# Strassen's seven half products for the output matmul of an attention and gated-MLP kernel

## The chip, the cores and the metric

The kernel runs on one core of one Trainium2 chip. The metric is the device time of the whole kernel in microseconds (us), taken as the median of several executions. Names used below: PE is the matmul engine (PEld is its loading of weights), DVE the vector engine, ACT the scalar engine, POOL the GpSimd engine, which here issues most loads, and SP the engine that issues stores and transposes by DMA. SBUF is the working memory, PSUM the accumulator memory of eight banks that PE writes.

## The reference

Attention with eight heads, three of which look at all earlier positions and five at a window of 64 and the first four positions, and then a gated feed-forward layer with a gated residual:

```python
# q, k, v: (4, 8, 768, 64) float32
scores = (q @ k.T) / 8, masked: causal for heads 0, 2, 6;
         causal and (window of 64, or key < 4) for heads 1, 3, 4, 5, 7
x = softmax(scores) @ v                    # as (3072, 512)

g   = gelu(x @ w_gate)                     # (512, 1536)
val = x @ w_val                            # (512, 1536)
ffn_out = (g * val) @ w_out                # (1536, 512)
res_gate = sigmoid(x @ w_res)              # (512, 512)
out = x + res_gate * ffn_out               # (3072, 512) float32
```

## The kernel before

The 3072 tokens are worked through in six chunks of four tiles of 128 tokens. Each chunk has an attention part (scores into PSUM, exponent on ACT, masks on DVE, weighting with v on PE, normalisation on DVE), a gate/value part, and an output part. The output part of one chunk is issued between the pieces of the next chunk's attention, so that PE always has something to do. The program is laid out by a list scheduler in the kernel's own Python: operations are added to a graph with a priority, and the scheduler decides the order on each engine and where the semaphore waits go. `HINTS` overrides single priorities, so a change of `HINTS` is a change of order.

The products are done in fp16 with fp32 accumulation. The gate/value part keeps its features transposed (features on the 128 partitions, tokens along the row), in a buffer `hT` of 12 feature blocks by 512 tokens, of which there are two:

```python
P_st = Pool(many("qks", 2, [128, 4096], FP16))     # raw q and k
P_er = Pool(many("er", 2, [128, 4608], FP16))      # exponents, heads with full attention
P_h = Pool(many("hT", 2, [128, NF, 512], FP16))    # features, NF = 12
P_ot = Pool(many("otile", 5, [128, D_MODEL], FP32))
# PSUM: kind: (how many at a time, banks)
    "av1": (3, one(0, 1, 6)), "av2": (1, [(0, 1)]),          # weighting
    "sc": (2, [(2, 3), (4, 5)]),                             # scores
    "gv": (4, one(6, 7, 5, 4, 3, 2)), "out": (2, one(6, 7)), # gate/value, output

# gate/value, for each feature block f (g and v: 4 matmuls of 512 columns each)
matmul(g[:, :], lhsT=w_gate[:, ci, f*128:(f+1)*128], rhs=xT[:, ci, :])   # ci = 0..3
matmul(v[:, :], lhsT=w_val [:, ci, f*128:(f+1)*128], rhs=xT[:, ci, :])
act:  gact = Gelu(g)
dve:  hT[:, f, :] = (gact * 0.5) * v
...
# output, for each of the chunk's four token tiles lt
matmul(rb, lhsT=xT[:, ci, s], rhs=wr[:, ci, :])            # residual gate, 4 x 512 columns
act:  sr = Tanh(0.5 * rb)
matmul(fb, lhsT=hT[:, fi, s], rhs=wo[:, fi, :])            # 12 x 512 columns
dve:  otile = (sr + 1) * fb                                # "gated"
dve:  otile = otile + xtok[:, lt, :]                       # "add"
sp:   out[rows] = otile
```

The last tile of the last chunk does its output product in column slices of 256, 128 and 128, so that its gating and store can begin earlier. While the first data are on their way, PE runs matmuls on a blank tile (line 1178), as many as the scheduler finds time for.

Of the kernel before, what the change touches and what calls it, by code (L numbers as in the profile page):

```python
# [4 lines left out]
NHEAD = 8  # L5
SEQ = 768
# [8 lines left out]
NCB = D_MODEL // 128  # L15
# [24 lines left out]
DT_FIRST = 2  # L40
DT_ALL = 9
# [5 lines left out]
    "0:-96.05 3:-32.5 13:-14.98 398:-205.14 399:-3161.01 400:-242.48 401:-60.67 406:194.11 428:585.68 "  # L47
    "430:523.84 442:461.16 444:1172.07 587:-105.78 592:-108.69 613:396.07 617:407.42 620:-11.7 640:556.2 "
    "642:106.88 643:194.09 646:-2979.21 649:-102.44 659:511.02 686:-2.88 687:77.5 695:496.52 696:499.45 "
    "698:-3129.77 703:60.14 704:-184.95 705:-133.38 707:183.02 708:380.49 711:7.46 712:149.85 713:-50.64 "  # L50
    "715:-14.97 722:1121.95 725:480.98 726:449.69 731:-39.24 732:60.67 733:-318.24 737:-43.72 738:419.39 "
    "739:143.85 743:67.93 744:-230.75 746:-318.2 749:428.99 755:137.07 756:5.66 757:60.69 761:-9.34 "
    "762:495.92 764:2489.99 778:1098.32 789:2479.4 791:2501.2 807:953.41 837:1156.8 842:1419.06 877:2567.99 "
    "879:1563.79 880:2429.98 883:2507.13 898:1013.73 933:1964.55 937:1029.47 939:1471.24 940:2476.14 "
    "955:3421 962:3506.26 963:3575.25 971:3584.03 984:2490.73 989:3565.66 1020:3589.17 1022:2520.47 "
    "1036:2494.69 1066:3486.98 1103:3422.44 1109:3530.5 1114:4315.61 1115:4410.02 1124:-926.78 1134:4596.47 "
    "1141:3465.41 1143:2510.98 1146:2495.35 1152:4653.43 1157:112.2 1170:3039.97 1193:107.93 1248:3488.54 "
    "1265:3479.95 1266:4395.47 1271:4430.01 1272:4484.04 1275:-26.92 1284:5420.01 1289:3472.11 1290:4444.38 "
    "1293:-34.14 1295:3453.61 1302:4490.78 1305:3510.02 1316:3998.02 1318:3550.85 1319:3550.87 1320:4107.35 "
    "1349:3529.55 1351:5429.99 1355:3583.42 1414:5485.04 1451:1066.16 1462:4552.31 1474:4473.03 1475:6343.89 "  # L60
    "1480:4497.31 1530:6505.9 1534:2349.36 1556:5501.98 1602:6498.99 1637:6513.87 1670:7448.62 1687:7406.44 "
    "1689:5504.27 "
# [399 lines left out]
def build_kernel(nc, q, k, v, w_gate, w_val, w_out, w_res, out):  # L462
# [15 lines left out]
    P_st = Pool(many("qks", 2, [128, 4096], FP16))  # L478
# [5 lines left out]
    P_er = Pool(many("er", 2, [128, 4608], FP16))  # L484
# [5 lines left out]
    P_h = Pool(many("hT", 2, [128, NF, 512], FP16))  # L490
# [7 lines left out]
        "av1": (2, one(0, 1)), "av2": (1, [(0, 1)]), "av1": (3, one(0, 1, 6)),  # L498
        "sc": (2, [(2, 3), (4, 5)]), "scr": (3, one(5, 4, 3, 2)), "scr0": (3, one(5, 4, 3, 2)),
# [148 lines left out]
    def loads_rows(c, si, b, a, z):  # L648

        n = z - a  # L650
        BB = batch(b)
        st = Buf(P_st)
        lo, hi = a * 128, z * 128
        base = {0: -60, 1: -15, 2: 50}[c]
        groups = ((0, 4), (4, 8)) if c == 0 else ((0, 8),)
        tok = {}

        def sv(j, h0, h1, w):
            return at(st)[:, :].rearrange("p (j h w) -> p j h w", j=2, h=NHEAD)[:, j, h0:h1, 0:w]
        for gi, (h0, h1) in enumerate(groups):  # L660
            for j, src in enumerate((q, k)):
                t = dma("pool", base + 4 * gi + j, (h1 - h0) * n * 0.089,
                        (lambda j=j, h0=h0, h1=h1: lambda: sv(j, h0, h1, n * 64))(),
                        src[b, h0:h1, lo:hi, :].rearrange("h (p j) d -> p h (j d)", j=n), bufs=[st])
                t.late = 1.2 if c else 0.0
                for h in range(h0, h1):
                    tok[j, h] = t
        values(b, a, z, base + (10 if c == 0 else 2), False, c == 0)

        per = 1 if c == 0 or n == 4 else 2  # L670
        for k_ in range(0, NPAIR, per):
            ps_ = ORDER[k_:k_ + per]
            pr = 1000 * c - 492 + ps_[0] if c else 40 * k_ - 205
            for js in (((1,), (0,)) if c == 0 else ((0, 1),)):
                scr = Buf(P_ps, "scr" if c else "scr0")
                items = [(p, jj) for jj in js for p in ps_]

                def tr(e, items=items, scr=scr):
                    return [e.transpose(out=at16(scr)[64 * x:64 * x + 64, (m * n + i) * 128:(m * n + i + 1) * 128],  # L679
                                        in_=at(st)[:, (jj * NHEAD + h) * 256 + i * 64:(jj * NHEAD + h) * 256 + (i + 1) * 64],  # L680
                                        identity=ident[:, :])
                            for m, (p, jj) in enumerate(items) for i in range(n) for x, h in enumerate(PAIRS[p])]
                tt = G.add("pe", c_mm(128, n) * len(items), tr, [t_ident] + [tok[jj, h] for p, jj in items for h in PAIRS[p]],
                           pr, bufs=[st, scr], name="qkT")
                tt.mode = "col"


                def ev(on, p0=ps_[0], scr=scr, j0=js[0], m=len(items)):
                    def fn(e):
                        o = at(BB.qkt)[:, :, :, lo:hi].rearrange("c j (y x) w -> c x (j y) w", x=2)[:, p0 % 2]  # L690
                        m0 = j0 * 2 + p0 // 2
                        o = o[:, m0:m0 + m, :].rearrange("c m (p j) -> c m p j", j=n)
                        i_ = at16(scr)[:, 0:m * n * 128].rearrange("c (m j p) -> c m p j", m=m, j=n)
                        return e.tensor_copy(out=o, in_=i_) if on == "dve" else e.activation(out=o, in_=i_, func=AF.Copy)
                    return fn
                w = n * 128 * len(items)
                t = G.flex({"dve": (c_dve(w), ev("dve")), "act": (c_act(w), ev("act"))}, [tt], pr,
                           bufs=[scr, BB.qkt], name="qkE")
                for p, jj in items:
                    for i in range(a, z):  # L700
                        (BB.ktok if jj else BB.qtok)[p, i] = t

    def loads_natural(c, si, b, a, z):
# [3 lines left out]
        st = Buf(P_st)  # L707
# [4 lines left out]
        for i in range(a, z):  # L712
            for j, src in ((1, k), (0, q)):
                def sv(i=i, j=j):
                    return at(st)[:, (j * 4 + i - a) * 512:(j * 4 + i - a + 1) * 512]
# [25 lines left out]
    def attention(c, segs, xbuf, xtbuf, xtoks, xttoks, l0=0, last=(), ek=None):  # L741
# [6 lines left out]
        for k_, p in enumerate(order):  # L748
# [34 lines left out]
            P.et = Buf(P_er if any(retr) else P_es)  # L783
            P.where, P.ready = {}, {}
            P.off = 0
            for g in range(0, len(banks), 2):
                scores(P, tiles, [t[1:] + (id(t[2]) in lower,) for t in banks[g:g + 2]], g, retr)
            todo.append(P)
# [295 lines left out]
    def gate_value(c, xtbuf, xttoks, halves=()):  # L1084
        h = Buf(P_h)
        toks = []
        ph(c, "table").append(G.add("act", 0.2, lambda e: e.activation(out=scratch[:, :], in_=ident[:, 0:1], func=AF.Gelu),
                                    [t_ident], 1000 * c - 100, fset="gelu", name="table"))
        for f in range(NF):
            pr = 1000 * c + 500 + f  # L1090
            if f < len(halves) * 2:

                ths = []
                for hf, deps in enumerate(halves):
# [11 lines left out]
                        out=at(h)[:, f, s], in0=at(ga)[:, 0:256], scalar=0.5, in1=at(vb)[:, 0:256], op0=ALU.mult, op1=ALU.mult))(),  # L1106
# [12 lines left out]
            for c0 in (0, 2):  # L1119
# [11 lines left out]
                out=at(h)[:, f, :], in0=at(ga)[:, :], scalar=0.5, in1=at(vb)[:, :], op0=ALU.mult, op1=ALU.mult))(),  # L1131
# [4 lines left out]

    TAIL = (slice(0, 256), slice(256, 384), slice(384, 512))

    def output(c, h, htoks, xbuf, xtoks, xtbuf, xttoks):
        segs = [(b, t) for (b, a, z) in CHUNKS[c] for t in range(a, z)]  # L1140
        for lt in range(4):
# [14 lines left out]
            for w in (TAIL if last else (slice(0, 512),)):  # L1156
                fb = Buf(P_ps, "gv" if last else "out")
                n = w.stop - w.start
                for j in range(6):
                    prev_t = G.add("pe", c_mm(n, 2), (lambda fb=fb, s=s, j=j, w=w: lambda e: [  # L1160
                        e.matmul(at(fb)[:, w], lhsT=at(h)[:, fi, s], rhs=wo[:, fi, w], start=(fi == 0), stop=(fi == NF - 1))  # L1161
                        for fi in range(2 * j, 2 * j + 2)])(),
                        [prev_t, wtok["o", j * 2 // 3], wtok["o", (2 * j + 1) // 3]] + htoks[2 * j] + htoks[2 * j + 1], pr,
                        bufs=[fb, h], name="ff")
# [24 lines left out]
    for c, segs in enumerate(CHUNKS):  # L1189
        xbuf, xtbuf, xtoks, xttoks = Buf(P_x), Buf(P_xt), {}, []  # L1190
        halves = []
        if c == 0:
            last, ek = (), Buf(P_ek)
            for l0 in (0, 2):
                halves.append([])
                last = attention(c, [(0, l0, l0 + 2)], xbuf, xtbuf, xtoks, halves[-1], l0, last, ek)
                xttoks.extend(halves[-1])
        else:
            attention(c, segs, xbuf, xtbuf, xtoks, xttoks)
        h, htoks = gate_value(c, xtbuf, xttoks, halves)  # L1200
        output(c, h, htoks, xbuf, xtoks, xtbuf, xttoks)
# [76 lines left out]
```

The softmax here doesn't subtract the row's maximum and nothing guards it: scores larger than these inputs give would overflow.

## Time and profile before

| what | value |
|---|---|
| time, median of 3 | 270.63 us (270.5 to 271.09) |
| span of the profiled execution | 268.8 us |
| granted clock of PE | 1.000 |
| first gate/value matmul | 19.6 us |
| last matmul issued by | 264.6 us |

Lines of the kernel that matter in the profile: 1116 is the gate/value product of 512 columns (1098 the same with 256, in the first chunk), 1146 the residual gate, 1161 the output product, 857 and 948 scores, 981, 991 and 1005 weighting, 1070 and 679 transposes, 1130 the features, 1165 "gated" and 1168 "add".

The slices of the span show a PE that is full from start to end, and DVE and ACT that go up in the attention parts and down in the gate/value parts. Each digit is the busy share of one fortieth of the span in tenths:

```profile
PE   8999999999999999999999999999999999999995
DVE  2698245485264376445476433486145367534344
ACT  3785358783334877136792243984233788233310
```

A matmul's record of 379 ns is the time from its start to its end; several are in flight at once, so the distance between starts has to be taken from the chain or from the timeline. Idle time of DVE and ACT costs nothing by itself.

### The profile page before, as it was taken

How to read it: one execution, taken by the hardware profiler on the slowest of the kernel's cores; microseconds unless marked ns; L12 is line 12 of the kernel's file. 1: busy time of each engine (PE TensorE's matmuls, PEld its weight loads, DVE VectorE, ACT ScalarE, POOL GpSimd, SP SyncE). 2: the span in 40 equal slices, each digit the busy share in tenths (PEclk: the TensorE clock that was granted, in tenths of full speed). 3: DMA queues.
4: the chain of work that ended last, by engine and by line, in shares of the span. 5: the costliest groups of instructions: out<-in, count | busy, mean ns of one | idle time of the engine just before them, and what ended most of it. 6: DMA issues, size and time to landing. Idle time of an engine off the chain costs nothing.

```text
span 268.8 us, 5676 instructions
## 1 busy us (share of the span) xinstructions
PE 264.2 (98%) x2391; PEld 138.7 (52%) x2391; DVE 140.1 (52%) x273; ACT 139.9 (52%) x215; POOL 87.3 (32%) x124
## 2 busy tenths in 40 slices
PE   8999999999999999999999999999999999999995
PEld 7677465465444455444455444555444455444444
DVE  2698245485264376445476433486145367534344
ACT  3785358783334877136792243984233788233310
POOL 8999508995808029894000000000000000000000
DMA  6999999999999999999994100022000113200013
GB/s 86 171 205 207 185 180 228 169 168 187 171 129 187 154 160 185 216 189 125 184 148 134 41 0 0 2 41 96 25 0 0 39 41 80 78 2 0 1 39 120
DMA packets 97562, 29.38 MB, mean 109 GB/s; under 512 B 85504, under 2 KB 93952, under 8 KB 97536
## 3 DMA queue, kind: packets, MB, share of 16 engines
q0 software_dynamic: 70320, 14.69, 65.5%
q1 hardware_dynamic: 27216, 14.33, 27.9%
q8 instruction: 19, 0.31, 0.5%
q14 instruction: 7, 0.06, 0.1%
HBM read 29.36 MB, written 6.29 MB: 133 GB/s over the span
## 4 chain that ended last, share of the span: by engine, by line
PE 93%; DMA 3%; POOL 1%; DVE 1%; issue 0%; POOLq 0%; DVEq 0%
PE ps L1116 44%; PE ps L1161 23%; PE ps L1146 8%; PE ps L857 5%; PE ps L991 3%; DMA va<-in_v_dram 3%; PE ps L1098 3%; PE ps L981 2%; PE ps L1005 2%; PE ps L1070 1%; POOL qks L555 1%; PE ps L948 1%; PE ps L679 1%; PE ps L1178 1%; DVE otile L1168 0%; DVE otile L1165 0%
## 5 line engine op out<-in xcount | busy, mean ns | idle before, releaser
L1130 DVE SCALAR_TENSOR_TENSOR hT<-gact,ps 128x512 f16<-128x512 f16 x68 | 45.8, 686 | 67.4 <-ACT gact L1128 36.6
L1128 ACT ACTIVATE gact<-ps 128x512 f16<-128x512 f32 x68 | 40.1, 597 | 74.0 <-PE ps L1116 72.5
L1116 PE MATMUL ps<-xT,wv 128*128 128x512 f16 x272 | 74.3, 379 | 0.0
L1116 PE MATMUL ps<-xT,wg 128*128 128x512 f16 x272 | 74.1, 379 | 0.0
L1161 PE MATMUL ps<-wo,hT 128*128 128x512 f16 (+2 forms) x312 | 70.4, 363 | 0.0
L1116 PEld LDWEIGHTS ps<-xT,wg 128*128 128x128 f16 x272 | 26.3, 98 | 31.5 <-ACT xT L1077 0.6
L1116 PEld LDWEIGHTS ps<-xT,wv 128*128 128x128 f16 x272 | 26.2, 98 | 30.5 <-DVE hT L1130 0.5
L1161 PEld LDWEIGHTS ps<-wo,hT 128*128 128x128 f16 x312 | 27.5, 98 | 27.0 <-issue 0.7
L873 ACT ACTIVATE er<-ps 128x1024 f16<-128x1024 f32 (+4 forms) x40 | 34.2, 891 | 9.5 <-PE ps L857 9.4
L555 POOL DMA_DIRECT2D qks<-in_k_dram x36 | 28.3, 827 | 32.4 <-DMA qkt<-qks 21.9
L555 POOL DMA_DIRECT2D qks<-in_q_dram x36 | 28.8, 840 | 0.8 <-POOLq L1260 0.8
L1165 DVE SCALAR_TENSOR_TENSOR otile<-srs,ps 128x512 f32<-128x512 f32 (+2 forms) x26 | 16.8, 644 | 16.5 <-PE ps L1161 16.4
L1146 PE MATMUL ps<-wr,xT 128*128 128x512 f16 x96 | 24.7, 379 | 0.0
L555 POOL DMA_DIRECT2D va<-in_v_dram x24 | 21.6, 926 | 2.7 <-PE ps L1005 2.7
L1149 ACT ACTIVATE srs<-ps 128x512 f32<-128x512 f32 x24 | 14.3, 597 | 15.6 <-PE ps L1146 15.3
L1048 DVE TENSOR_TENSOR xtok<-ps,rcp 128x512 f32<-128x512 f32 (+1 forms) x28 | 16.9, 609 | 0.6
L1168 DVE TENSOR_TENSOR otile<-otile,xtok 128x512 f32<-128x512 f32 (+2 forms) x26 | 16.8, 647 | 0.7
L857 PE MATMUL ps<-qkt 64*128 64x64 f16 (+4 forms) x391 | 16.9, 213 | 0.0
L857 PEld LDWEIGHTS ps<-qkt 64*128 64x128 f16 x391 | 9.8, 94 | 9.4 <-issue 3.4
L873 ACT ACTIVATE es<-ps 128x1024 f16<-128x1024 f32 (+1 forms) x14 | 12.6, 898 | 2.9 <-PE ps L857 2.6
L1146 PEld LDWEIGHTS ps<-wr,xT 128*128 128x128 f16 x96 | 8.7, 98 | 10.0 <-issue 0.7
L1178 PE MATMUL ps<-blank 128*128 128x128 f16 x116 | 11.4, 249 | 1.1 <-DVE blank L527 1.1
(70 smaller groups left out, 212.5 us busy)
## 6 DMA issues: line engine op xcount, KB each, us to landing
out_dram<-otile SPq DMA_DIRECT2D x23, 256.0 KB, 2.2
va<-in_v_dram POOLq DMA_DIRECT2D x24, 128.0 KB, 17.0
qks<-in_k_dram POOLq DMA_DIRECT2D x32, 64.0 KB, 11.9
qks<-in_q_dram POOLq DMA_DIRECT2D x32, 64.0 KB, 12.4
wg<-in_moe_w_gate_dram POOLq DMA_DIRECT2D x3, 512.0 KB, 10.3
wv<-in_moe_w_val_dram POOLq DMA_DIRECT2D x3, 512.0 KB, 10.6
wo<-in_moe_w_out_dram POOLq DMA_DIRECT2D x4, 384.0 KB, 22.2
vs<-va SPq DMA_DIRECT2D x4, 260.0 KB, 7.4
```

Source lines behind the costliest of these rows:

```text
L555: return G.add(eng, issue, lambda e: e.dma_start(out_ap(), in_ap), deps, prio, bufs=bufs, dma=cost, name=name, grp=grp)
L857: return [e.matmul(at(scr)[:, oo:oo + w], lhsT=side(BB, low, 1)[half, k0:k0 + 128], rhs=side(BB, low, 0)[half, qq:qq + w], start=True, sto ...
L873: return e.activation(out=o, in_=i_, func=AF.Exp, scale=SM_SCALE)
L1048: t2 = G.add("dve", c_dve(2 * n * 64), lambda e: e.tensor_tensor(out=xview(), in0=avv(0, DHEAD), in1=scale(), op=ALU.mult), [t1] + xdeps, ...
L1116: return lambda e: [e.matmul(at(dst)[:, :], lhsT=w[:, ci, f * 128:(f + 1) * 128], rhs=at(xtbuf)[:, ci, :], start=(ci == 0), stop=(ci == NC ...
L1128: ta = G.add("act", c_act(512), (lambda gb=gb, ga=ga: lambda e: e.activation(out=at(ga)[:, :], in_=at(gb)[:, :], func=AF.Gelu))(), [tg], p ...
L1130: th = G.add("dve", c_dve(512), (lambda vb=vb, ga=ga, f=f: lambda e: e.scalar_tensor_tensor(out=at(h)[:, f, :], in0=at(ga)[:, :], scalar=0 ...
L1146: e.matmul(at(rb)[:, :], lhsT=at(xtbuf)[:, ci, s], rhs=wr[:, ci, :], start=(ci == 0), stop=(ci == NCB - 1))
L1149: ta = G.add("act", c_act(512), (lambda rb=rb, sr=sr: lambda e: e.activation(out=at(sr)[:, :], in_=at(rb)[:, :], func=AF.Tanh, scale=0.5)) ...
L1161: e.matmul(at(fb)[:, w], lhsT=at(h)[:, fi, s], rhs=wo[:, fi, w], start=(fi == 0), stop=(fi == NF - 1))
L1165: t1 = G.add("dve", c_dve(n), (lambda fb=fb, sr=sr, ot=ot, w=w: lambda e: e.scalar_tensor_tensor(out=at(ot)[:, w], in0=at(sr)[:, w], scala ...
L1168: t2 = G.add("dve", c_dve(n), (lambda ot=ot, lt=lt, w=w: lambda e: e.tensor_tensor(out=at(ot)[:, w], in0=at(ot)[:, w], in1=at(xbuf)[:, lt, ...
```

## The change

What it does and what it is for. Take two token tiles as the two rows of a 2 x 2 block matrix, even and odd feature blocks as its columns, and the output weights as a 2 x 2 block matrix of even and odd feature blocks by left and right 256 output columns. The block product then needs eight half products. The change uses Strassen's scheme in Winograd's form, which needs seven, with sums of blocks made beforehand. A half product is 6 matmuls of 256 columns. So a pair of tiles takes 42 matmuls of 256 columns in place of 24 of 512. It is for less work on PE, in exchange for work on DVE and ACT. Nine of the twelve pairs are done so: both pairs of chunks 1 to 4 and the first pair of chunk 5 (`FAST`).

Sums of the weights are made once (four differences, 1536 elements a row each), sums of the features in each chunk (four, in two groups of feature blocks). One of the feature sums, S3, replaces the block it is made from. Two PSUM banks, X and Y, take the seven products; X keeps accumulating products while its partial sums are copied out ("keep"), and the others are added from Y ("plus").

```diff
+FAST = (1, 2, 3, 4, 5)
 HINTS = ( ... every number of it is new ... )

-    P_st = Pool(many("qks", 2, [128, 4096], FP16))
+    P_st = Pool(many("qks", 3, [128, 2048], FP16))
-    P_er = Pool(many("er", 2, [128, 4608], FP16))
+    P_ea = Pool(many("ea", 1, [128, 4608], FP16))
+    P_eb = Pool(many("eb", 1, [128, 2816], FP16))
-    P_h = Pool(many("hT", 2, [128, NF, 512], FP16))
+    P_h = Pool(many("hT", 1, [128, NF, 4, 128], FP16))
+    P_hs = Pool(many("hS", 1, [128, 3, NF // 2, 2, 128], FP16))
+    wt = sb("wt", [128, 4, NF // 2, 256], FP16)
-        "av1": (2, one(0, 1)), "av2": (1, [(0, 1)]), "av1": (3, one(0, 1, 6)),
-        "sc": (2, [(2, 3), (4, 5)]), ...
+        "av1": (3, one(0, 1, 6)), "av2": (2, [(0, 1), (4, 5), (2, 3)]),
+        "sc": (3, [(2, 3), (4, 5), (0, 1)]), ...

+    def sums(c, h, htoks):                       # dve; two groups of feature blocks, 4 + 2
+            t1 = add(0, (0, 1), (1, 1), ALU.add, deps, "s1")
+            t2 = add(1, 0, (0, 0), ALU.subtract, [t1], "s2")
+            t4 = add(2, (1, 0), 1, ALU.subtract, [t2], "s4")
+            t3 = add((0, 1), (0, 0), (0, 1), ALU.subtract, [t1], "s3")   # in place
+    def weight_sums():                           # dve; four differences
+        t1 = add(0, w(0, 1), w(0, 0), tall)
+        t2 = add(1, w(1, 1), wt[:, 0], [t1])
+        add(2, w(1, 1), w(0, 1), tall)
+        add(3, w(1, 0), wt[:, 1], [t2])

+    def output_fast(c, pi, h, htoks, hs, stoks, xbuf, xtoks, xtbuf, xttoks):
+        ... residual gate and Tanh of both tiles, as before ...
+        X, Y = Buf(P_ps, "out"), Buf(P_ps, "out")
+        # a product: 6 x  matmul(D[:, 0:256], lhsT=left(j), rhs=right(j))
+        p1 = product(X, "A11", "B11", True, [])
+        k1 = keep(p1, 0, 0)                      # copy of X to otile, DVE or ACT
+        p2 = product(Y, "A12", "B21", True, [])
+        c11 = plus(p2, k1, 0, 0)                 # otile += Y, DVE
+        p6 = product(X, "S2", "T2", False, [k1]) # on top of p1
+        k2 = keep(p6, 0, 256)
+        p5 = product(Y, "S1", "T1", True, [c11])
+        p7 = product(X, "S3", "T3", False, [k2])
+        k3 = keep(p7, 1, 256)
+        c22 = plus(p5, k3, 1, 256)
+        p4 = product(X, "A22", "T4", False, [k3])
+        p3 = product(Y, "S4", "B22", False, [c22])
+        c12 = plus(p3, k2, 0, 256)
+        ... gated: one piece of 512 (first tile), two of 256 (second tile, one from X);
+        ... add and store as before ...
```

Beside the products, the change has one feature buffer where there were two, one buffer for each kind of exponents, the raw q and k in three smaller buffers (q and k of the first chunk apart), bank pairs of PSUM that scores and weighting share, and a new order throughout.

## The prediction

> **What bounds the kernel now.** I read the page's busy shares first, then the waits of PE, then the chain of waits in order of time, then stretches of the span, and last the groups by form for the durations.
>
> ```profile
> span 268.8 us, 5676 instructions
> PE 264.2 (98%) x2391; PEld 138.7 (52%) x2391; DVE 140.1 (52%) x273; ACT 139.9 (52%) x215; POOL 87.3 (32%) x124
> PE 93%; DMA 3%; POOL 1%; DVE 1%; issue 0%; POOLq 0%; DVEq 0%
> ```
>
> PE is busy 98% of the span and makes up 93% of the chain that ended last. Busy time alone would not settle it, since matmuls overlap; the waits of PE (us in total, times, longest) do:
>
> ```profile
> PE ps L1178 <- DVE blank L527: 1.1, 1, 1.1
> PE ps L991 <- DMA va<-in_v_dram: 0.4, 1, 0.4
> PE ps L679 <- DMA qks<-in_q_dram: 0.2, 1, 0.2
> ```
>
> All three lie in the start. After the first gate product at 19.6 us, PE waits for nobody. So the time is the start (19.6), plus PE's own throughput for 245 us, plus a tail of 4.2 us after the last matmul at 264.6. The chain in order of time (start, us, what) gives that throughput:
>
> ```profile
> 19.59 1.75 PE ps L1098 x16
> ...
> 45.23 0.86 PE ps L1146 x4
> 46.43 0.97 PE ps L1146 x4
> ...
> 231.29 20.72 PE ps L1116 x96
> ```
>
> 96 matmuls of 512 columns in 20.72 us are 215.8 ns each; 16 matmuls of 256 columns in 1.75 us are 109.4 ns each. A run of four 512-column matmuls takes 0.86 us, and 0.97 us where it borders on matmuls that use part of the array: about 0.1 us for a change of array shape.
>
> The room of the vector engine (columns: stretch, us, then busy time and count of PE, PEld, DVE, ACT, POOL), for an attention stretch and for the gate/value stretch after it:
>
> ```profile
> 129.50:148.20 18.70, 18.70 (x203) 9.53 (x202) 12.09 (x23) 11.13 (x16) 0.00 (x0) 1.00 0.98 152
> 148.20:168.90 20.70, 20.70 (x111) 9.37 (x110) 7.92 (x13) 8.15 (x13) 0.00 (x0) 1.00 0.04 13
> ```
>
> DVE has 6.6 us free in the first and 12.8 us in the second; neither it nor ACT is a bound. The mean durations used below (busy us, mean ns):
>
> ```profile
> L1161 PE MATMUL ps<-wo,hT 128*128 128x512 f16 x276 | 67.6, 379 | 0.0
> L1161 PEld LDWEIGHTS ps<-wo,hT 128*128 128x128 f16 x312 | 27.5, 98 | 27.0 <-issue 0.7 <-DVE hT L1130 0.4
> L1165 DVE SCALAR_TENSOR_TENSOR otile<-srs,ps 128x512 f32<-128x512 f32 x23 | 15.8, 686 | 15.7 <-PE ps L1161 15.6
> L1165 DVE SCALAR_TENSOR_TENSOR otile<-srs,ps 128x256 f32<-128x256 f32 x1 | 0.4, 422 | 0.8 <-PE ps L1161 0.8
> L909 DVE TENSOR_TENSOR es<-es,m_win 128x1024 f16<-128x1024 f16 x10 | 6.7, 680 | 4.3 <-ACT es L873 4.3
> L909 DVE TENSOR_TENSOR er<-er,m_causal 128x512 f16<-128x512 f16 x7 | 2.9, 418 | 0.9 <-ACT er L873 0.9
> L1102 ACT ACTIVATE gact<-ps 128x256 f16<-128x256 f32 x8 | 2.9, 382 | 3.5 <-PE ps L1098 3.5
> ```
>
> **What the skill says.** The Trainium skill, "TensorE: Matmul & The Clock Gate", section "Wait — 56ns, not 53.3ns?", gives a warm start-to-start of N/2.4 + 2.5 ns: 215.8 for 512 and 109.2 for 256 columns. The trace agrees (215.8, 109.4), and shows that halving the columns costs almost nothing per column. The same page, "Step-by-step: what each phase is for", has the next weight load run while the matmul before it streams. A load takes 98 ns here, under the 109.4 ns of a half product, and the 16 matmuls at 109.4 ns each had a load of their own: it hides, with 11 ns to spare. "VectorE: DVE Perf Modes", "The perf-mode tier table", puts a two-tensor operation at double rate for 16-bit SBUF operands and single rate for fp32 or PSUM. The trace agrees: 1024 fp16 elements in 680 ns, 512 fp32 in 686. "PSUM — Partial Sum Buffer", "The four PSUM rules", allows a synchronised read of a partial sum within an accumulation group; the change rests on it, and the kernel before has no case of it.
>
> **The change, part by part.**
>
> *Products.* A pair of token tiles takes 2 x 12 matmuls of 512 columns now: 24 x 215.8 = 5.18 us. Seven products of 6 matmuls of 256 columns take 42 x 109.4 = 4.59 us. That is 0.58 us less per pair. Nine of the twelve pairs change (two in each of chunks 1 to 4, one in chunk 5): 378 half matmuls replace 216 whole ones, saving 46.61 - 41.35 = 5.3 us, all on the path. Changes of array shape do not become dearer: in the two instruction orders I count 88 of them after the first gate product before, 90 after.
>
> *Start.* The order of the changed kernel issues 126 matmuls on the blank tile before the first gate product, against 116, and moves 12 small weighting matmuls ahead of it. The identity comes later on POOL, behind a memset and two mask steps. Q, K, V and weight loads keep their sequence in one saturated queue, so they should land as before. Five blank matmuls at 17.79 us end 0.44 us later and one alone takes 0.22, so each further one costs about 0.06 us; ten make 0.6. I put the start at +0.5 us.
>
> *Vector work added.* Sums of features: four of 1024 fp16 elements and four of 512 per full chunk, 4 x 0.68 + 4 x 0.42 = 4.4 us, and 2.8 us in chunk 5 with half the size: 20.4. Four weight differences of 1536 elements, by extrapolation 0.95 us each: 3.8. In the nine pairs 27 adds of 256 columns from PSUM at 0.42: 11.3. Of 27 copies the order puts 17 on DVE (7.1) and 10 on ACT (3.8). Gating in three pieces for two: 9 x 0.15 = 1.4. DVE rises by 44 us to 184 (69% of the span), ACT to about 144. None of this is on the path by itself.
>
> *Tail of the last chunk.* Here no attention work separates the products. By the order: whole product, residual, p1, residual, p6, p2, p7, p5, p4, p3, residual, last tile. Each product of 0.65 us must be followed by a copy or add of its bank before that bank is written again. From the end of PE's issue to the start of the reader is about 0.27 us now (last matmul of a tile issued by 262.2, gating at 262.48); then 0.38 to 0.42, then a wake-up of some 0.04. That is 0.7 us against 0.65 beside it: 0.05 to 0.1 us short, three or four times. The first p1 waits for the bank of the whole product, whose gating stands on DVE behind the seven last feature sums: 0.35 us. The p2 bank waits for the second tanh (0.27 + 0.60 + 0.05 against 0.65): 0.25. The last residual waits for the gating of p4: 0.2. Together about 0.9 us, which is more than the 0.58 that this pair saves.
>
> *One feature buffer.* The next chunk's first feature tile may be written only after the last product that reads the old ones. In the order, at most one product is left when the next gate products start, and those fill PSUM first. Cost: near 0, at most 0.2 us a chunk.
>
> *Shared bank pairs.* PE does not wait for scores or weighting banks before, so more pairs remove no wait; they only give the order room.
>
> *Attention stretches.* From the last feature tile of chunk 1 to the first of chunk 2, DVE's order is 4 sums, 5 copies, 5 adds, 5 masks, 4 reciprocals, 6 normalisations, 5 gatings, 3 residual adds, 1 transpose copy: 18.6 us by the durations above (reciprocal 0.2). PE has about 17.5 us of work there (18.7 less 2 x 0.58), and about 3 us of gate products before DVE's next feature tile: DVE is some 90% full, where it was 12.1 of 18.7. It issues in order, and PE waits for five or six of its results per stretch. I put this at 0.25 us per stretch, four times: 1.0 us, my least certain term.
>
> Sum: -5.3 + 0.5 + 0.9 + 1.0 = -2.9, and 270.6 - 2.9 = 267.7. The order looks laid out so that attention work stands between almost all products, so I lean a little lower: **267.4 us**.
>
> **The rivals.** (a) PE alone: every new wait is filled, and the whole 5.3 us arrives: 265.3. For it: PE's waits are nil now, and the new order interleaves; against it: the last chunk has nothing to interleave with. (b) The vector engine becomes the bound of the attention stretches: one to two us lost in each of four, giving back everything: 270 to 273. For it: 90% full; against it: adds of the residual and the first group of sums can slide into the gate stretch, where DVE has 12.8 us free. (c) Weight loads: 42 instead of 24 per pair. Break-even is 5.18/42 = 123 ns per half matmul; the trace's 109.4 with a load each speaks against it. With 123 the time would be about 273. (d) The start loses more, because the later identity delays the first transposes: up to +1.5.
>
> **Range and chances.** A gain of over 2% needs 5.4 us, more than the whole saving of PE; only a better start could give it. A loss of over 2% needs rival (b) at its worst. Range 265.4 to 270.4: its low end is (a), its high end half of (b).
>
> **What would show it.** PE's half products at 109 ns start to start (right) or above 115 (rival c). The chunk 1 to 4 attention stretches about 1 us shorter on PE; if they are as long as before, with PE waiting for copies and adds, (b) holds. The stretch from the last gate/value matmul to the last matmul no shorter than 12.6 us (from 252.0 to 264.6): the last pair's term. The first gate product after 20 us: the start's term. Wrong altogether if PE waits for feature or exponent buffers at chunk borders.

## The result, and the profile after

| | before | after |
|---|---|---|
| time, median | 270.65 us | 277.11 us (276.67 to 277.44) |
| ratio, 95% interval | | 1.0239 [1.0224, 1.0254] |
| span of the profiled execution | 268.8 us | 274.9 us |

The change makes the kernel 2.4% slower, and the time lies outside the predicted range. The page of the changed kernel, the same lines as before (busy shares, three rows of the forty slices, the chain of waits by engine):

```profile
span 274.9 us, 6145 instructions
PE 262.7 (96%) x2563; PEld 154.7 (56%) x2563; DVE 175.1 (64%) x362; ACT 146.0 (53%) x233; POOL 87.2 (32%) x124
...
PE   7999999999997299999999999999999999999995
...
PEclk9999999999999579999999999999999999999999
DMA  6999999999999999999952120002210004110013
...
PE 81%; DMA 10%; POOL 3%; DVE 2%; SPq 2%; issue 1%; POOLq 0%
```

DVE rose to 64% of the span and ACT stayed at 53%. The new thing is a hole in PE's row in slices 13 and 14 (82 to 96 us), with a dent in the clock at its end (a 5 and a 7 among nines), and a tenth of the chain that is now DMA. The waits of PE (us in total, times, longest):

```profile
PE ps L879 <- DMA q<-qkt: 7.3, 1, 7.3
PE ps L1313 <- DVE blank L538: 1.1, 1, 1.1
PE ps L696 <- POOL ident L524: 0.5, 1, 0.5
PE ps L1013 <- DMA va<-in_v_dram: 0.3, 1, 0.3
```

The last three belong to the start, as before. The first is one single wait of 7.3 us: scores of chunk 2 wait for `q<-qkt`. This is a copy by DMA (line 749) that moves q and k of one head from the upper 64 partitions to the lower ones, for the four tiles of chunk 2; I call it the q6 copy, after its buffer (the expectations below say "Q copy of tile 6" for it). The chain of waits through that stretch (start, us, what; SPq is the queue of instructions on SP, and "issue" is time for which the profile shows no wait):

```profile
64.59 1.74 POOL va L566 x2
66.33 15.79 DMA va<-in_v_dram
...
82.21 0.47 SPq L649
...
82.72 1.61 SPq L741
...
84.37 1.40 SPq L741
...
85.81 1.37 SPq L741
...
87.49 6.85 DMA q<-qkt
94.34 0.35 issue
94.69 1.01 PE ps L879 x10
95.70 1.85 PE ps L1208 x4
97.55 1.28 PE ps L1229 x6
```

From the top down: POOL may load V of batch 2 from 64.6 us, the load lands at 82.1, and only then can SP issue its next instruction, the shift copy of that V (line 649; it moves V by 64 tokens for the window heads). Batches are counted from 0 and hold six tiles each, so this V is the third of four, and chunk 3 is the first to read it, after 138 us. Behind it on SP stand three transposes of q and k (line 741) and then the q6 copy, which is issued at 87.49 and lands at 94.34. SP took its instructions in order and issued nothing from 76.2 to 82.1 us, so everything behind the shift copy stood still, needed or not. The waits of SP's own queue between 58 and 92 us show the block:

```profile
SPq L420 <- DMA va<-in_v_dram: 5.9, 1, 5.9
```

In the kernel before the shift copy of batch 2 stands far behind the q6 copy, and was issued at 92.76: the q6 copy was issued at 80.81, landed at 87.58, and PE read it first at 89.1. The rows of the copy's buffer in the kernel before (after the colon the shortest, median and longest duration in ns, then first and last start), and the time from the copy's issue to its landing:

```profile
L857 PE MATMUL ps<-q x3: 216/279/323, 89.1 to 91.6; 64*128 64x384 f16 x1, 64*128 64x128 f16 x1, 64*128 64x256 f16 x1
L730 SPq DMA_DIRECT2D q<-qkt x1: 667/667/667, 80.8 to 80.8; - x1
...
DMA to landing us min/median/max: 6.8/6.8/6.8
```

So before there was a margin of 1.5 us (89.1 - 87.58). The new order wants the copy at about 87.4, 1.7 us sooner, and has it 6.8 us later.

The last two lines of the chain show a second loss. Four products of 512 columns took 1.85 us (0.97 and 0.86 in the chain before), and a half product 1.28. The clock by stretch (columns: stretch, length, busy time and count of PE, PEld, DVE, ACT, POOL, then the granted clock of PE; the last two are not used):

```profile
89.00:89.90 0.90, 0.00 (x0) 0.00 (x0) 0.90 (x3) 0.00 (x0) 0.00 (x0) 1.00 2.14 148
90.00:100.00 10.00, 5.30 (x44) 2.85 (x45) 1.09 (x3) 3.12 (x4) 5.93 (x8) 0.50 1.72 196
100.20:103.00 2.80, 2.80 (x47) 1.93 (x47) 0.75 (x3) 1.43 (x3) 0.00 (x0) 1.00 1.85 159
```

While PE waits, at 89.9, its clock falls to one half, and it stays there until 100.2: 5.5 us of work at half speed, 2.7 us lost. The Trainium skill, "TensorE: Matmul & The Clock Gate", section "What's actually happening", has the half clock after an idle window of about 3.4 us and the full one after about 3.4 us of sustained work; here the fall comes 2.5 us after the end of the last matmul (87.4), earlier than the page has it, and the recovery after 5.5 us of work.

Where the 6.2 us of span come from, stage by stage. Each row runs from the start of the last gate/value matmul of one chunk to that of the next, read from the traces; the last column, slack2, is the final version of the experiments below (e11):

| stretch, us | before | after | slack2 |
|---|---|---|---|
| start to chunk 0 | 44.85 | 45.19 | 45.90 |
| chunk 0 to 1 | 41.92 | 41.82 | 41.82 |
| chunk 1 to 2 | 42.32 | 51.38 | 42.90 |
| chunk 2 to 3 | 40.76 | 39.76 | 39.76 |
| chunk 3 to 4 | 39.80 | 39.22 | 39.14 |
| chunk 4 to 5 | 41.98 | 40.41 | 40.41 |
| chunk 5 to the end | 17.13 | 17.16 | 17.18 |

One stretch loses 9.06 us; the three after it gain 1.00, 0.58 and 1.57, which is 3.15 together. The rest is under 0.4.

### The profile page after: what moved, and what is told of

It is laid out like the page before. It is cut to its first block, busy times and chain, and to the rows that moved or that the text cites. A ratio compares the mean times of both kernels' runs of the same rounds, so it can differ in the third digit from the quotient of the medians.

```text
span 274.9 us, 6145 instructions
## 1 busy us (share of the span) xinstructions
PE 262.7 (96%) x2563; PEld 154.7 (56%) x2563; DVE 175.1 (64%) x362; ACT 146.0 (53%) x233; POOL 87.2 (32%) x124
## 4 chain that ended last, share of the span: by engine, by line
PE 81%; DMA 10%; POOL 3%; DVE 2%; SPq 2%; issue 1%; POOLq 0%
PE ps L1139 35%; PE ps L1229 15%; DMA va<-in_v_dram 8%; PE ps L1208 6%; PE ps L879 5%; PE ps L1296 4%; PE ps L1013 3%; PE ps L1121 3%; DMA q<-qkt 2%; PE ps L1003 2%; PE ps L1027 2%; SPq L741 2%; PE ps L1281 2%; PE ps L1092 1%; POOL va L566 1%
## 5 line engine op out<-in xcount | busy, mean ns | idle before, releaser
L1139 PE MATMUL ps<-xT,wg 128*128 128x512 f16 x272 | 70.6, 379 | 0.0
L895 ACT ACTIVATE ea<-ps 128x1024 f16<-128x1024 f32 (+2 forms) x24 | 21.0, 915 | 5.9 <-PE ps L879 5.6
L1208 PE MATMUL ps<-wr,xT 128*128 128x512 f16 x72 | 19.3, 396 | 0.0
L879 PEld LDWEIGHTS ps<-qkt 64*128 64x128 f16 x391 | 10.3, 97 | 14.4 <-issue 12.0
L895 ACT ACTIVATE eb<-ps 128x1024 f16<-128x1024 f32 (+3 forms) x16 | 13.3, 858 | 8.9 <-PE ps L879 8.9
L1242 DVE TENSOR_TENSOR otile<-otile,ps 128x256 f32<-128x256 f32 x27 | 11.2, 417 | 10.3 <-PE ps L1229 8.5
L1296 PE MATMUL ps<-wo,hT 128*128 128x512 f16 (+2 forms) x96 | 16.9, 326 | 0.0
L1236 DVE COPY otile<-ps 128x256 f32<-128x256 f32 x17 | 7.1, 420 | 13.9 <-PE ps L1229 13.8
L1229 PE MATMUL ps<-wo,hT 128*128 128x256 f16 x108 | 15.5, 281 | 0.1
L1229 PE MATMUL ps<-wt,hT 128*128 128x256 f16 x108 | 15.1, 273 | 0.0
L1229 PE MATMUL ps<-wt,hS 128*128 128x256 f16 x108 | 14.9, 273 | 0.0
```

Of the source, the lines that this page charges most:

```text
L879: return [e.matmul(at(scr)[:, oo:oo + w], lhsT=side(BB, low, 1)[half, k0:k0 + 128], rhs=side(BB, low, 0)[half, qq:qq + w], start=True, sto ...
L895: return e.activation(out=o, in_=i_, func=AF.Exp, scale=SM_SCALE)
L1139: return lambda e: [e.matmul(at(dst)[:, :], lhsT=w[:, ci, f * 128:(f + 1) * 128], rhs=at(xtbuf)[:, ci, :], start=(ci == 0), stop=(ci == NC ...
L1208: e.matmul(at(rb)[:, :], lhsT=at(xtbuf)[:, ci, s], rhs=wr[:, ci, :], start=(ci == 0), stop=(ci == NCB - 1))
L1229: e.matmul(at(D)[:, 0:256], lhsT=left[l](j), rhs=right[r](j), start=first and j == 0, stop=(j == NF // 2 - 1), skip_group_check=True) for ...
L1242: return G.add("dve", c_dve(256), lambda e: e.tensor_tensor(out=dst(), in0=dst(), in1=at(Y)[:, 0:256], op=ALU.add), [t, k], pr, bufs=[Y, o ...
```

## The experiments

Two theories. **Q:** the changed order put the shift copy ahead of the q6 copy in SP's queue; the wait and the slow clock after it are the whole loss, and with the order mended the predicted gain shows. Against it stands the rival that the products, the single feature buffer or DVE's extra work are what costs (the expectations call it theory V). **D** was formed after the first four runs, because mending the order did not bring what Q says: up to about 140 us, when the last inputs have landed, the DMA engines are busy 90% or more of the time (nines in the DMA row up to slice 20), the needs that DMA feeds have small margins (1.5 us at the q6 copy before), and a PE that has become faster runs into the next of them.

Every edit moves instructions in one engine's order after the scheduler has run; waits are then assigned anew. `behind((a, b), c)` takes a and b out and puts them behind c. Numbers are the program's instruction groups: 476 the q6 copy, 491 the first half of the shift copy, 469, 475, 479 and 495 transposes on SP, 792 an output store, 1065 the DMA transpose of chunk 2's features (`xT`), 961 a residual, 965 and 966 the first half product, 1023 and 1027 the first two score groups of chunk 2. Times of one kernel are given as median and range, as several of these versions vary by some us from execution to execution. The ratios to before leave out executions that lie more than 1.5% above the fastest of the same version, while the medians and ranges take in all. A profile shows one execution, whose time is given where it stands far from the median.

**1. Mend the order on SP** (e2), and the shift copy alone (e1).

```diff
+    behind((491,), 476)     # e1 and e2
+    behind((469,), 475)     # e2
```

> The changed kernel, with two entries of SP's queue moved and nothing else: the early shift copy of the third batch's values goes behind the copy of q and k to the lower partitions, and one late transpose goes back to its place. Theory Q (order in SP's queue): that shift copy waits for values that land at 82.1 us and holds everything behind it; with it moved, the copy of q and k is issued near 80.5 us and lands near 87, when PE needs it. The wait of 7.3 us goes, and with it the slow clock after it (about 2.6 us): 277.1 - 9.9 = 267.2 us, granted clock 1.00. Theory V (the vector engine or the single buffers hold the attention stretches, and the long wait only hides it): most of the time comes back as waits for DVE or for buffers later on, 272 us or more.

> As the run before, but only the shift copy is moved; the late transpose stays late. Its landing at 81.9 us then sets when the copy of q and k can start. Theory Q: issued near 82.0, landed near 88.5, so a wait of about 1 us stays on PE, too short to slow the clock: 268.2 us. Theory V: as above, 272 or more.

e2: 271.97 us (271.5 to 273.71), ratio to before 1.0045 [1.0028, 1.0063]. e1: 271.35 us (268.08 to 274.61, 20 executions), ratio 0.9988 [0.9969, 1.0007]. The 7.3 us wait is gone in both, and with it 5 to 6 us, but both miss their expectation by 3 to 5 us. PE's waits in e2:

```profile
PE ps L1139 <- DMA xT<-x: 3.6, 1, 3.6
PE ps L879 <- DVE hS L1173: 1.4, 1, 1.4
```

The second is still the q6 copy: it landed at 88.39 and PE went on at 88.74, after the same 0.35 us as in the changed kernel, while the DVE sum that is named ended at 88.75, too late to have released it. The first is new: the gate/value products of chunk 2 wait for the transpose of their inputs by DMA. In the chain:

```profile
102.40 10.33 DMA xT<-x
```

It was issued at the same time as before, but landed at 112.73; before it landed at 109.39 and nobody waited. From 113.2 to 116.7 us the clock was then one half, another 1.7 us. (This execution took 273.71 us, the longest of the five.) In the profile of e1 the same transpose took 8.1 us instead of 10.3 and nobody waited for it; that execution had a span of 269.0, and the q6 copy cost 2.0. So Q names the cause of most of the loss in the changed kernel, and is not enough for the prediction's 267.

**2. The same fault in the kernel before** (b1): its shift copy moved ahead of its q6 copy, nothing else.

```diff
+    behind((491,), 479)
```

> The kernel before, with the shift copy put early in SP's queue as in the changed kernel, and nothing of the change. Its values land at 84.0 us there, so the copy of q and k is issued near 89 instead of 80.8 and lands near 95.5 instead of 87.6. Theory Q: PE waits 4 to 7 us for it and loses 1 to 2.5 us more to a slow clock: 276 to 280 us from 270.65. Theory V: the kernel before, with two feature buffers and little work on DVE, has other work for PE and stays within 1 us of 270.65.

280.06 us (279.01 to 280.89), ratio 1.0341 [1.0313, 1.0369]. The first of PE's waits:

```profile
PE ps L857 <- DMA q<-qkt: 7.2, 1, 7.2
```

A kernel without half products, with two feature buffers and DVE at 52%, gets the same wait from that one move and loses 9.4 us. So the order on SP is enough for this loss, without the new products. That the products, the buffer and DVE do not cost is what the later stretches of the table above show, which gain 3.15 us with all of them in place.

**3. Keep PE's clock up during the wait** (e3): 100 matmuls on the blank tile ahead of the waiting scores of the changed kernel.

> The changed kernel with SP's queue as it is, and 100 matmuls on the blank tile put on PE just ahead of the score matmuls that wait (5.6 us of work in a wait of 7.3 us; their result is overwritten). The wait stays. If the slow clock after the wait comes from PE being idle, the clock stays at 1.00 and the 2.6 us of slow matmuls go: 274.5 us. If the clock falls for another reason, 277.1 stays; if the fill delays the scores, it is longer.

278.53 us (277.93 to 281.4), ratio 1.0307 [1.0252, 1.0363]: not faster. In its profile the fill ran from 88 to about 94, a wait of 3.1 us followed, and the clock was one half from 96.5 to 99.9, for 3.4 us in place of 10.2: 1.4 us of work were lost to it instead of 2.7. Less idling, less half clock; the clock did not stay at 1.00, as the fill did not cover the whole wait. But the start was 1.1 us later in that execution, and the q6 copy was issued 1.3 us later and took 8.2 us instead of 6.9 to land. Whether the fill itself delayed it is open; as a remedy it is of no use.

**4. Take the next DMA need away** (e5a, e5b): on top of e2, what transpose 1065 did is done by PE, into banks 2 and 3, with copies by DVE. It is half of chunk 2's inputs: two of four blocks of 128 columns of `x`, each in four token tiles, so eight small transposes (the expectations speak of four blocks of eight). e5b moves one score group as well.

```diff
+    G.prog["sp"].remove(xd)                       # 1065, DMA transpose
+    tp = Task("pe", ..., 4 x transpose(128 columns) into bank 2 or 3, ...)   # twice
+    te = Task("dve", ..., tensor_copy(xT[:, cb, 0:512], bank), ...)          # twice
+    behind((1023,), 966)                          # e5b only
```

> The version with the shift copy and the DMA transpose back in their old places on SP (271.97 us) still lost 3.6 us of PE waiting for the DMA transpose of chunk 2's features (xT) and about 1.7 us of half-speed matmuls after it. Here four of chunk 2's eight feature blocks (those of that one transpose) are transposed by TensorE (eight 128-column transposes, two copies by VectorE) in place of the DMA. Theory D (the first half is paced by the saturated DMA queues; each DMA-fed need that PE now reaches early costs its wait and some half-speed matmuls): the xT wait and its slow matmuls go, 8 transposes cost 0.45: 271.97 - 3.6 - 1.7 + 0.45 = about 267. Rival: the queues are simply full, and another transfer's wait of 2 us or more takes the place of this one: 270 or above.

> As the run before it, and the first scores of chunk 2, which wait for the padded copy of Q of tile 6, are issued behind a residual and the first half product, so that the copy has about 1 us more. Theory D: of the 1.4 us wait at these scores 1 us goes: about 266.0, the sum of PE's own saving without any stall. Rival (the wait only moves to the next need): no better than the run before it, within 0.3 us.

e5a: 273.07 us (272.64, 274.09, 267.86 and 273.5). e5b: 269.36 us (267.63 to 272.75, 22 executions), ratio 0.994 [0.9918, 0.9963]. Both medians miss what D expects, e5a by 6 us and e5b by 3.4; only the lowest executions come near it. Neither profile has a wait for `xT`. In the profile of e5a the q6 copy costs 2.9 us of waiting and then a clock of 0.7 for a slice, in that of e5b 0.6 us and nothing more; that one, at 267.67 us among the shortest of the 22, shows a span of 265.9, 2.8 us under before. The move in e5b was badly chosen: of the two score groups only 1023 went back, while 1027, which reads the same copy, stayed in front, so the copy had hardly more time. How much of the difference between e5a and e5b is the move, and how much is that between executions, in which the copy lands now sooner and now later (90.99 and 87.77 in the two profiles), is not shown.

**5. Less for the queues to carry** (e6): e2 with 8 of the 16 loads of q and k of chunk 3 left out. Chunk 3 is then computed from stale data, so only the time is of use.

> The version with the old SP order (271.97 us), with 8 of the 16 Q and K loads of chunk 3's tiles left out (2 MB or less that the queues carry while chunks 1 and 2 run; the kernel then computes chunk 3 from stale data, so only its time is of use). Theory D: the queues empty sooner, the Q copy of tile 6 and the transpose xT land 1 to 3 us earlier, PE's waits for them shrink: about 269. Rival (landing times are set by the issue order on SP and a fixed latency, not by the load on the queues): unchanged, 272 within 0.7.

268.90 us (267.62 to 272.56), ratio 0.9918 [0.9898, 0.9938], as theory D expects and 3.1 us under e2. The transpose landed at 109.05 in place of 112.73, and nobody waited for it; but of these 3.7 us 2.4 come from an earlier issue on SP (100.01 against 102.40) and only 1.3 from a shorter way to its landing. The q6 copy did not land sooner (89.23 against 88.39), and PE's wait for it was 1.0. So the loads of a chunk whose attention PE reaches only after 130 us cost some 3 us in chunks 1 and 2. Whether they do so by the bytes that they carry, as D says, or by the issues of POOL and SP (POOL had 8 fewer, and SP's transposes waited less for data), this run does not separate.

**6. Without the last chunk's pair** (e7): as e5b, with whole products in chunk 5.

```diff
-FAST = (1, 2, 3, 4, 5)
+FAST = (1, 2, 3, 4)
```

> As the version with transposes on TensorE and later scores, but the last chunk's pair is computed with whole products again, so that four chunks keep the seven half products. Prices the tail: the pair saves 0.58 us of products and paid 0.50 us of PE waits in the trace of the changed kernel, so without it 0.1 us slower, within 0.4. If the prediction's own tail term (0.9 of waits) was right: 0.3 us faster.

271.48 us (268.15 to 274.95), ratio 0.9978 [0.9954, 1.0001]. The medians do not answer the question, as the profile of e7 (273.38 us) has 2.8 us of waiting for the q6 copy and that of e5b 0.6. The end of the span, behind all DMA waits, says more: from the last gate/value matmul to the end e7 needs 17.53 us and e5b 17.18. But the order is not the same: the hints for that part go by number and are left out in e7, and PE waits there twice for 0.18 us (a residual begun at 257.80 takes 0.86, and the product behind it begins at 258.84; likewise at 262.48). Without these 0.36 the two are level, as are the changed kernel with 17.16 and the kernel before with 17.13. So the last pair gains next to nothing.

**7. Slack for the q6 copy** (e8), the same with the DMA transpose kept (e9), and the changed kernel with only the q6 copy moved (e10).

```diff
+    behind((476, 792), 495)         # e8, e9: q6 copy up, a store down, on top of e2
+    behind((1023, 1027), 966)       # e8, e9: both score groups behind a half product
+    behind((962,), 1049)            # e8, e9: Tanh of that residual first on ACT
+    (1065 to PE, as in e5a)         # e8 only
+    behind((476,), 479)             # e10 only, on the changed kernel
```

> Slack on both sides of the Q copy of tile 6, with four feature blocks of chunk 2 transposed on TensorE as before: on SP the copy goes ahead of one transpose and of an output store that stood before it (1.2 us earlier), and both score groups of chunk 2 that read it (in the run called 'later' one of the two had stayed in front) are issued 1.6 us later, behind a residual and the first half product. Theory D (the loss is a matter of margins at the DMA-fed needs): no PE wait for the copy in the profile, no slow clock, about 267.0 in the median (265.9 of span in the one stall-free profile, plus 1.7 between span and time, less or more 0.7 for the start), and the runs lie close together (within 1.5 us instead of 5). Rival (the first half is bound by what the queues carry, however it is ordered): the wait moves to the next DMA-fed need, 269 to 271, spread as wide.

> The same slack for the Q copy, but chunk 2's features transposed by the DMA as in the changed kernel. If the DMA transpose is a need of its own with too small a margin (it landed 112.7 us for a use at 109.1 in the version with only SP's order mended, without a wait in the other), PE waits 1 to 4 us for xT and the time is 1 to 5 us above the version with TensorE transposes; if the xT wait came only from the late Q copy before it, both are within 0.5 us.

> The changed kernel with one instruction moved and nothing else: the Q copy of tile 6 stands ahead of the shift copy on SP. In the changed kernel the last transpose it needs landed at 81.9, so it can issue at about 82 instead of 87.5. Theory Q (SP's in-order queue held the copy behind the shift copy): wait 7.3 to about 2, slow clock 2.6 to about 1: 277.1 - 5.3 - 1.6 = about 270. Rival (the copy is late for another reason, its own transposes or the load on the queues): the wait stays above 5 and the time above 274.

e8: 269.17 us (268.69 to 270.3, 6 executions), ratio 0.9935 [0.9912, 0.9958]. e9: 271.59 us (269.19 to 275.95), ratio 0.9989 [0.9963, 1.0015]. e10: 274.86 us (274.31 to 277.13), ratio 1.0158 [1.0123, 1.0193]. The longest of PE's waits in e10:

```profile
PE ps L1139 <- DMA xT<-x: 4.7, 1, 4.7
...
102.94 10.70 DMA xT<-x
```

This is the next need of theory D at its clearest (the second line is from the chain). One instruction moved, and the wait of 7.3 us for the q6 copy is gone altogether (it was issued at 81.77 and landed at 88.08). But 4.7 us come back 20 us later, at the transpose `xT`, which was issued at 102.94 and landed at 113.64; with the half clock after it (113.4 to 116.8 us), 277.11 - 274.86 = 2.25 us are left of a saving that should have been about 7. My expectation of 270 counted the first wait and did not look for the next. e9 shows the same need, with the slack: 2.3 us of waiting for `xT`, 2.4 us slower than e8 in the medians and 1.5 by the ratios. In e8 the waits of PE list none for the q6 copy or for `xT`; besides two at the start there are:

```profile
PE ps L879 <- ACT eb L895: 1.1, 1, 1.1
PE ps L1208 <- DVE hT L1153: 0.4, 1, 0.4
```

The margin is still thin: in this execution the q6 copy landed at 90.01, and PE stood for 0.13 us until 90.15. Its executions lie within 1.6 us of each other, about as D expects. The median, in the range that the rival gave, missed D's 267.0 by 2.2, of which 1.1 and 0.4 are waits that my own move made: with both score groups behind the half product, nothing covers the first exponent.

**8. The last version** (e11): the first score group between the residual and the half product.

```diff
-    behind((1023, 1027), 966)
+    behind((1027,), 961)
+    behind((1023,), 966)
```

> As the version with slack on both sides of the Q copy (269.17 us), whose profile has no DMA wait in chunk 1 but two waits of its own making, 1.1 us for an exponent and 0.4 for a feature tile. Here the first score group goes out between the residual and the first half product, and only the second behind them, so that the products cover the first exponent. Theory D: the 1.1 goes, about 268.0, still within 1.5 us from lowest to highest. Rival (the copy then stalls PE again, as the first group reads it 0.7 us earlier): 269 or more and a spread of several us.

268.88 us (267.95 to 270.12, 8 executions), ratio to before 0.9941 [0.9922, 0.996]: faster than both kernels, by 0.6% and 3.0%. The wait for the exponent fell from 1.1 to 0.2, no wait for the q6 copy came back (it landed at 86.14 and was first read at 89.49), and the median still gained only 0.3, with a range of 2.2 us where 1.5 was expected. The profiled execution began its first gate product 0.9 us later than that of e8 (21.10 against 20.22), with a wait for V and one for `xtok` at the start:

```profile
PE ps L1013 <- DMA va<-in_v_dram: 0.3, 1, 0.3
PE ps L879 <- ACT eb L895: 0.2, 1, 0.2
PE ps L1013 <- DVE xtok L1070: 0.2, 1, 0.2
```

Why the start of this family differs by up to 0.9 us between executions while the copies are in the same order is open.

## Why the prediction was wrong

The sum had the right terms for PE and none for DMA.

**The step that failed** is that the sum counts no wait for a transfer. Its only ground is the sentence in the term of the start, "Q, K, V and weight loads keep their sequence in one saturated queue, so they should land as before". For POOL's loads that held (the V load that the shift copy waits for landed at 82.12, before at 83.96), and it was taken to hold for all transfers of the kernel. The copies and transposes on SP were never looked through, although the change says "a new order throughout" and the order is visible without a run: the shift copy of batch 2 stands ahead of the q6 copy. The missing term is +7.3 of waiting (the 0.35 between landing and next matmul are part of it) and +2.7 of slow clock. Rivals (c) and (d) looked at other engines; no rival had a transfer that lands late. The remark "PE waits for nobody" led there: a wait of zero in the kernel before says nothing of its margin, which was 1.5 us at this copy.

**Products, -5.3.** Right in kind and size. In full-clock stretches a half product takes 0.66 us in the chain (109 ns for each of six). From chunk 2 to chunk 5, three stretches with two pairs each should save 3 x 1.16 = 3.48 and save 3.15. Chunk 1's pairs lie inside the stretch that lost 9.06: 7.3 + 2.7 - 1.16 is 8.8, which leaves 0.2 open, so their saving is not seen by itself. In slack2 that stretch should take 42.32 - 1.16 + 0.45 (eight transposes) + 0.6 (two waits) = 42.2 and takes 42.90; these 0.7 us are unexplained.

**Attention stretches, +1.0.** Too large: the three stretches give back 0.33 of 3.48, against 0.75 predicted for three. It is not that DVE has more room than predicted: in the attention part of chunk 3 it is 90% full, as foreseen (columns as above):

```profile
138.80:155.10 16.30, 16.30 (x240) 11.99 (x239) 14.65 (x35) 12.32 (x20) 0.00 (x0) 1.00 0.26 67
```

But behind the start the list of the waits of PE has none for a result of DVE (those at the tail, below, are too short for it): a DVE that is 90% full held up nobody in these stretches, and rival (b) was wrong.

**Start, +0.5.** The first gate product began at 20.29 in place of 19.43, and the last gate/value matmul of chunk 0 came 0.34 later. About right.

**Tail of the last chunk, +0.9 of waits.** Too large (its parts add up to 0.95 to 1.2 as they stand there). From the last gate/value matmul to the end the changed kernel needs 17.16 us and the kernel before 17.13, so what is lost there eats the 0.58 that the pair saves and hardly more. Five products of the last pair, p6, p2, p7, p5 and p4 (timeline of PE in the changed kernel; start, us, then the line):

```profile
264.04 0.82 PE L1229 MATMUL ps<-wt,hS 128*128 128x256 f16 x6
264.89 0.83 PE L1229 MATMUL ps<-wo,hT 128*128 128x256 f16 x6
265.56 0.82 PE L1229 MATMUL ps<-wt,hT 128*128 128x256 f16 x6
266.23 0.83 PE L1229 MATMUL ps<-wt,hS 128*128 128x256 f16 x6
266.91 0.83 PE L1229 MATMUL ps<-wt,hT 128*128 128x256 f16 x6
```

Six matmuls at 109.4 ns are 0.66. The last four start 0.67 apart where 0.70 to 0.75 was predicted, so those small waits did not come. The three others did, and were shorter: p1 waited 0.18 in place of 0.35 (the residual before it began at 261.45 and takes 0.86; p1 began at 262.49), p2 0.19 in place of 0.25 (264.04 + 0.66 = 264.70, begun at 264.89), the last residual 0.13 in place of 0.2 (p3 began at 267.58, the residual at 268.37). Together they are 0.50. The predicted marker of 12.6 us for this stretch, and the "last matmul issued by 264.6" behind it, were misread: the chain before leaves PE at 264.6, but matmuls go on until about 266, so the end of the span is what can be compared.

**One feature buffer and shared bank pairs, 0.** No wait for them shows in the changed kernel. **The sum without DMA:** 0.34 - 0.10 - 1.16 - 3.15 + 0.03 is -4.0, where -1.16 is what chunk 1's pairs should save and not a measurement. The one profile that came nearest to it, that of e5b, with eight extra transposes (0.45) and 0.6 of waiting, is 2.8 us under before. So "267.4" was about right for PE's side of the work, some 1 us too cautious, and wrong for the kernel, since in the first half PE does not set the pace alone.

## What to carry to other kernels

Before an engine that runs without waits is made faster, measure the margins of everything it reads from DMA: landing time against first use. Here a margin of 1.5 us became a wait of 7.3 when the order changed. An engine that issues its transfers in order has a schedule of its own: compare its order instruction by instruction, ask of each entry what it waits for, and put an early-ready copy that someone needs ahead of one whose data come late.

## What the runs showed of the hardware

A wait of PE can cost more than its length. After waits of 7.3, 3.6 and 4.7 us (changed kernel, e2, e10) the half clock took 2.7, 1.7 and 1.6 us more. A wait of 2.0 us (in e1), shorter than the window of 3.4 us that the skill's page names, was followed by 3.4 us at half clock, 1.7 us lost; but one of 2.3 us (in e9, 110.2 to 112.6) and one of 1.1 us (in e8) left the clock at full. So the length alone does not decide, and what else does is not shown here. The half clock lasted 3.41 us in e1, e2, e3 and e10, and 10.24 us, three times as long, in the changed kernel and in b1.

The time from issue to landing of the same DMA transpose, issued between 102 and 107 us, was 5.4 us in the changed kernel, 6.1 in e9, 7.0 in the kernel before, 8.1 in e1, 10.3 in e2 and 10.7 in e10. What stands ahead of it on SP has a part in this. In all fourteen traces the transfers that SP issued between 50 and 130 us landed in the order of their issue. In e2 and e10 the transpose was issued 1.6 and 1.3 us behind another one, which landed only at 109.23 and 110.41, and landed 3.5 and 3.2 us after that one; in the changed kernel SP's issue before it lay 6.6 us back and landed 1.5 us after the transpose was issued. Why the transposes ahead of it took 8.4 us and more in e2 and e10, and 6.7 in the kernel before, was not settled.

The 0.1 us that the prediction gives to a change of array shape falls on one side only. In the kernel before, a residual's four matmuls take 0.96 us up to the next matmul where that one uses part of the array (4 of 4), but 0.87 where they come behind such matmuls (5 of 5); of the fifteen others one takes 0.95 and the rest 0.86.

The spread of some versions, 6.5 us over 20 executions of e1 against 1.6 for e8, goes with the clock: in e1 the seven executions above 272 us have a mean clock of 0.994 or less, and twelve of the thirteen others 0.999 or more. Which transfer PE waited for in them is not known. What was not tried is a third buffer for V, which would let the load that held up SP start sooner.
